# RWKV-5 attention and a mixture of depths on one core: k loads on ScalarE's queue, the first chosen rows a step later, the last rows in parts

## The chip, the cores and the metric

One core of a Trainium2 chip runs the whole program as a single launch. The metric is the device time of that launch in microseconds, the median of several runs; beside it stands one profiled execution, from which all rows below come.

## The reference, cut to what matters

```python
# attention: r, k, v are (B=4, H=8, S=768, D=48), w and u are (8, 48)
for t in range(S):
    cur = einsum('bhd,bhe->bhde', u * k[t], v[t])
    y[t] = einsum('bhd,bhde->bhe', r[t], state + cur)
    state = w * state + einsum('bhd,bhe->bhde', k[t], v[t])
x = y.transpose(0, 2, 1, 3).reshape(B, S, 384)
# mixture of depths, for each batch b
scores = x[b] @ w_gate
top = argpartition(-scores, 128)[:128]            # capacity 128 of 768 rows
ye = maximum(x[b, top] @ w1, 0) @ w2              # 384 -> 1024 -> 384
out[b] = x[b]
out[b, top] = x[b, top] + sigmoid(scores[top])[:, None] * ye
```

## The kernel before

The sequence is cut into units of 128 tokens, six to a batch, 24 in all. A loop over `i` from 1 to 24 is a software pipeline: in step `i` TensorE (PE) finishes the rows of unit `i-1` (`states_part`, `values_part`), makes the state sums and scores of unit `i` (`state_sums`, `scores`) and turns k and r of unit `i+1` with the identity (`turn_k`, `turn_r`). GpSimd (POOL) does four elementwise products in each step (`scaled` of unit `i+2`, `diagonal` of `i+1`, two in `bonus` of `i+2`). VectorE (DVE) masks and sums, ScalarE (ACT) copies PSUM to SBUF (`leave_y`, `turned_k`) and scales the states (`decays`). The order on each engine is the order in which the code is written; no scheduler moves anything.

Loads: `load(n, which)` issues DMAs from HBM. One unit's k or r is one DMA of 192 KB in runs of 192 bytes; v is two DMAs of 96 KB for units 0 to 9 and one after that. Step `i` loads k and r of unit `i+4` and v of unit `i+3`, all on SyncE's queue (SP), which also carries the stores of finished rows (`store_y`, 384 KB for two units). k has four buffers, r four, v five. The expert weights `w1` and `w2` come in eight DMAs of 384 KB on ScalarE's queue in steps 7 to 14 (`weights`).

Mixture of depths: a batch's scores are turned into places by comparisons; `one_hot` and `pick` give the 128 chosen row numbers, `picked` writes them as `idx`, `fetch` gathers the rows from HBM (`xr`, an indirect DMA of POOL), `chosen` turns them on PE, `chosen_copy` brings them to SBUF (`xt`). Then eight `hidden` and eight `expert` pieces are queued, and `pieces(m)` takes `m` of them at three places of each later step (table `FIRST` for batch 0, `STEP` for the others). `leave` makes the gated sum, `store_rows` scatters the rows. For batch 0, `fetch` stands at the end of step 9, and `chosen` near the end of step 10. The last batch has no later steps: its expert runs alone behind the loop, the tail.

The row numbers 0 to 127 that `one_hot` compares with are read from `slots`, columns 384 to 511 of the PSUM bank `PE` (tile `e`), into whose other columns `hidden` writes:

```python
slots = PE[:, Dm : Dm + 128]
nc.vector.tensor_tensor(OH[b, z], q[:, :, None].to_broadcast([128, NC, 128]),
                        slots[:, None, :].to_broadcast([128, NC, 128]), op=OP.is_equal)
```

Of the kernel before, what the change touches and what calls it, by code (L numbers as in the profile page):

```python
# [7 lines left out]
F32 = mybir.dt.float32  # L8
# [9 lines left out]
def kernel(  # L18
# [84 lines left out]
    kpad = const.tile([128, H, PAD], F32, name="kpad")  # L103
    KIN, VIN = {}, {}

    def load(n, which):
        if n >= NU:
            return
        b, c = divmod(n, NC)
        rows = slice(c * T, (c + 1) * T)  # L110
        if "k" in which:
            KIN[n] = kpad[:, :, :D] if n == 0 else work.tile([128, H, D], F32, name="kin", bufs=NIN)
            nc.sync.dma_start(out=KIN[n], in_=k[b, :, rows, :].rearrange("h t d -> t h d"))
        if "r" in which:
# [349 lines left out]

    def one_hot(b, z):
        OH[b, z] = work.tile([128, NC, 128], BF16, name="oh")
        if z:
            q = work.tile([128, NC], F32, name="qz")
            nc.vector.tensor_scalar(q, QQ[b], float(-128 * z), None, op0=OP.add)
        else:  # L470
            q = QQ[b]
        nc.vector.tensor_tensor(OH[b, z], q[:, :, None].to_broadcast([128, NC, 128]),  # L472
                                slots[:, None, :].to_broadcast([128, NC, 128]), op=OP.is_equal)

# [45 lines left out]
    def chosen(b, z):  # L520
        for d in range(KD):
            nc.tensor.transpose(rows_bank(b, z)[:, d * 128 : (d + 1) * 128],
                                XR[b, z][:, d * 128 : (d + 1) * 128], ident)

    def chosen_copy(b, z):
        XT[b, z] = work.tile([128, KD, 128], F32, name="xt", bufs=NST + 1)
        nc.scalar.copy(XT[b, z], rows_bank(b, z)[:, :Dm].rearrange("d (k t) -> d k t", k=KD))  # L527

# [6 lines left out]
    def hidden(b, z, f):  # L535
# [5 lines left out]
        for d in range(KD):  # L541
            nc.tensor.matmul(out=pe[:, (f - f0) * 128 : (f - f0 + 1) * 128], lhsT=w1[:, d, f * 128 : (f + 1) * 128],  # L542
                             rhs=XT[b, z][:, d, :], start=(d == 0), stop=(d == KD - 1))
        if f == f1 - 1:
            nc.scalar.activation(HT[b, z][:, f0:f1, :],
                                 pe[:, : (f1 - f0) * 128].rearrange("f (a t) -> f a t", a=f1 - f0), AF.Relu)

    def expert(b, z, f):
# [50 lines left out]
    NONE = (0, 0, 0)  # L599
    FIRST = NONE, (1, 1, 1), (1, 1, 1), (1, 1, 1), (1, 1, 1), (0, 2, 2)  # L600
    STEP = NONE, (2, 1, 1), (1, 1, 1), (1, 1, 1), (1, 1, 1), (0, 2, 1)
    counts = {}
    for b in range(B - 1):
# [3 lines left out]
        for z in range(NST):  # L607
# [3 lines left out]
            at(e + 4, "pool", fetch, b, z)  # L611
            at(e + 5, "chosen", chosen, b, z)
            at(e + 5, "chosen copy", chosen_copy, b, z)
            at(e + 5, "queue", enqueue, b, z)
            at(e + 5, "gate", gates, b, z)
        for j, m in enumerate(STEP if b else FIRST):
# [21 lines left out]
    nc.vector.tensor_mul(wc, tr[:, 1, :, C], tr[:, 1, :, C])  # L638
    load(3, "kr")
    bonus(0)  # L640
# [176 lines left out]
```

## Time and profile before

| what | value |
|---|---|
| median of 3 runs (lowest to highest) | 171.22 us (170.57 to 174.28) |
| time of the profiled execution | 170.33 us |
| its span, first to last instruction | 168.5 us |
| busy share of the span: PE, DVE, POOL, ACT | 88%, 64%, 62%, 48% |
| DMA: share of the 16 engines, SP's queue (q1) and ACT's (q10) | 51.9% and 6.6% |
| PE clock in the 40 slices | 0.9 or more, but for slices 11 (0.7), 12 (0.8), 15 (0.7) and 16 (0.5), counted from 1: `9999999999789975999999999999999999999998` |

The profiled execution stands 0.89 us below the median, and its span 1.83 us below its own time. Times in rows count from the start of the span. A name such as `SPq` or `ACTq` means the queue's own sequencer, which issues DMAs. Steps are found by their PE instructions: `L361` and `L368` are the state sums, `L319` the scores, `L333` the rows y, `L428` the score transpose that follows them, `L522` the transposes of chosen rows, `L542` a `hidden` piece (six records), `L549` an `expert` piece (two records).

### The profile page before, as it was taken

What the parts mean: (1) busy time and instruction counts of PE and PEld (TensorE: products, weight loads), DVE (VectorE), ACT (ScalarE), POOL (GpSimd) and SP (SyncE); (2) the same over time, 40 slices, a digit from 0 to 9 for tenths busy, and PEclk for the clock granted to TensorE, in tenths of its full rate; (3) what the DMA queues carried; (4) which work ended last, traced back from release to release, by engine and by line L of the source; (5) the groups of instructions that cost most, each with busy time, mean ns of one, the idle gap of its engine ahead of it and who ended that gap; (6) DMA issues with size and microseconds to landing.
All of it is one profiled execution on the core that took longest, in us unless ns stands there. A gap on an engine that the chain in (4) does not pass through costs nothing.

```text
span 168.5 us, 8206 instructions
## 1 busy us (share of the span) xinstructions
PE 147.5 (88%) x3531; PEld 115.2 (68%) x3532; DVE 107.4 (64%) x325; ACT 80.1 (48%) x279; POOL 103.9 (62%) x135
## 2 busy tenths in 40 slices
PE   6899998898598849999999989999998887698970
PEld 2587886686486639888676778877757767558730
DVE  6889888779367681667787766677877656402010
ACT  3286778657255443546455547464555453002200
POOL 7689989888806796178645997876559700022001
PEclk9999999999789975999999999999999999999998
DMA  5997888798999799879977778492201221011001
GB/s 121 173 188 151 176 160 214 141 228 198 239 221 233 180 223 222 209 197 241 297 201 156 144 173 184 91 218 53 92 9 53 97 93 51 2 47 47 4 0 49
DMA packets 81715, 24.33 MB, mean 144 GB/s; under 512 B 75533, under 2 KB 81294, under 8 KB 81678
## 3 DMA queue, kind: packets, MB, share of 16 engines
q1 hardware_dynamic: 78320, 18.88, 51.9%
q10 hardware_dynamic: 2846, 3.35, 6.6%
q0 software_dynamic: 512, 1.57, 3.0%
q8 instruction: 28, 0.46, 1.1%
q14 instruction: 9, 0.07, 0.2%
HBM read 18.29 MB, written 5.51 MB: 141 GB/s over the span
## 4 chain that ended last, share of the span: by engine, by line
PE 42%; issue 23%; POOL 11%; DMA 11%; DVE 4%; SPq 4%; ACT 2%; POOLq 1%; DVEq 0%
PE y L333 9%; PE e L542 7%; PE rp L319 6%; DMA vw<-in_v_dram 5%; PE e L549 4%; PE rp L361 4%; DMA xr<-out_dram,idx 4%; SPq L121 3%; POOL rku L248 2%; PE pk L282 2%; POOL at L263 2%; POOL rk L246 2%; DMA vin<-in_v_dram 2%; PE rp L368 2%; PE pk L278 2%
## 5 line engine op out<-in xcount | busy, mean ns | idle before, releaser
L263 POOL TENSOR_TENSOR at<-dia,du 128x512 f32<-128x512 f32 (+2 forms) x24 | 23.2, 967 | 23.7 <-DVE du L253 13.3
L542 PE MATMUL e<-xt,w 128*128 128x128 f32 x162 | 24.8, 296 | 3.0 <-DVE oh L472 1.3
L248 POOL TENSOR_TENSOR rku<-rk,ub 128x384 f32<-128x384 f32 x24 | 24.1, 1004 | 2.7 <-DMA ub<-in_u_dram 0.9
L542 PEld LDWEIGHTS e<-xt,w 128*128 128x128 f32 x162 | 20.6, 198 | 4.9 <-ACT xt L527 1.4
L246 POOL TENSOR_TENSOR rk<-rpad,kin 128x384 f32<-128x384 f32 x23 | 23.1, 1003 | 0.0
L397 ACT COPY x<-y 128x192 f32<-128x192 f32 x23 | 7.4, 320 | 30.2 <-PE y L333 30.1
L240 POOL TENSOR_TENSOR kw<-kin,wk 128x384 f32<-128x384 f32 x21 | 21.1, 1003 | 0.1
L383 ACT ACTIVATE z<-g,wc 128x48 f32<-128x48 f32 x80 | 20.1, 322 | 0.0
L319 PE MATMUL rp<-rh,kh 48*64 48x64 f32 x768 | 18.4, 232 | 0.8 <-issue 0.7
L319 PEld LDWEIGHTS rp<-rh,kh 48*64 48x64 f32 x768 | 14.8, 141 | 5.5 <-issue 2.5
L333 PEld LDWEIGHTS y<-z,rh 48*64 48x64 f32 x704 | 13.7, 138 | 6.4 <-ACT x L399 1.7
L324 DVE COPY_PREDICATED at<-mask,rp 128x512 f32<-128x512 uint32 x24 | 17.5, 729 | 0.5 <-POOL at L263 0.5
L333 PE MATMUL y<-z,rh 48*64 48x48 f32 x704 | 16.7, 226 | 0.1
L375 DVE TENSOR_TENSOR z<-rp,z 128x192 f32<-128x192 f32 x20 | 7.1, 356 | 15.2 <-PE rp L319 10.7
L501 POOL DMA_INDIRECT xr<-out_dram,idx x4 | 4.1, 1036 | 18.2 <-DVE idx L483 18.2
L253 DVE TENSOR_REDUCE du<-rku 128x8 f32<-128x384 f32 x24 | 13.1, 545 | 2.2 <-POOL rku L248 2.1
L549 PE MATMUL e<-w,ht 128*128 128x384 f32 x32 | 13.7, 526 | 0.3 <-DVE oh L472 0.3
L416 DVE SCALAR_TENSOR_TENSOR scr<-x,m 128x384 f32<-128x384 f32 x24 | 13.1, 548 | 0.7 <-ACT x L399 0.7
L564 POOL DMA_INDIRECT out_dram<-ot,idx x4 | 4.0, 1010 | 15.0 <-DVE ot L555 14.7
L444 DVE TENSOR_SCALAR_CACHE_REDUCE gt<-srow,sc 128x128 bf16<-128x128 f32 (+4 forms) x20 | 12.2, 609 | 0.0
L333 PE MATMUL y<-vin,at 64*64 64x48 f32 x448 | 10.3, 224 | 1.5 <-ACT tiny L346 1.2
L313 DVE TENSOR_TENSOR rh<-pr,tr 128x256 f32<-128x256 f32 x14 | 5.9, 420 | 8.9 <-PE pr L282 8.9
(134 smaller groups left out, 300.9 us busy)
## 6 DMA issues: line engine op xcount, KB each, us to landing
rpad<-in_r_dram SPq DMA_DIRECT2D x24, 192.0 KB, 4.2
kin<-in_k_dram SPq DMA_DIRECT2D x23, 192.0 KB, 4.4
out_dram<-x SPq DMA_DIRECT2D x11, 384.0 KB, 5.1
w<-in_moe_w_dram ACTq DMA_DIRECT2D x8, 384.0 KB, 4.6
vin<-in_v_dram SPq DMA_DIRECT2D x14, 192.0 KB, 4.8
vw<-in_v_dram SPq DMA_DIRECT2D x20, 96.0 KB, 3.4
out_dram<-x SPq DMA_DIRECT2D x2, 192.0 KB
kpad<-in_k_dram SPq DMA_DIRECT2D x1, 192.0 KB
```

What stands on the lines that cost most here:

```text
L240: engine.tensor_mul(kws[n % NKW][:, :, :D], KIN[n], wk)
L246: nc.gpsimd.tensor_mul(rk, rpads[n % NIN][:, :, :D], KIN[n])
L248: nc.gpsimd.tensor_mul(RKU[n], rk, ub)
L253: nc.vector.tensor_reduce(DU[n], RKU[n].rearrange("t (p i) d -> t i p d", i=2), axis=AX.X, op=OP.add)
L263: nc.gpsimd.tensor_mul(AT[n][:, :m], dia[:, None, :].to_broadcast([128, m, C]), DU[n].rearrange("t i p -> t (i p)")[:, :m, None].to_broadc ...
L319: nc.tensor.matmul(out=RP[half(c), i, hp * C : (hp + 1) * C], lhsT=KH[n][head(i), hp, half(c)], rhs=RH[n][head(i), hp, half(c)], start=Tru ...
L324: nc.vector.copy_predicated(at, causal, RP[:, :, : NP * C].rearrange("s i (p t) -> s i p t", p=NP))
L333: nc.tensor.matmul(out=y_out(hp, i, c), lhsT=lhsT, rhs=rhs, start=(n, i, c) not in begun, stop=True, skip_group_check=True)
L383: nc.scalar.activation(state(n + 1)[:, hp, 0, :], G[n][:, hp, :], AF.Copy, scale=wc[:, hp : hp + 1])
L416: nc.vector.scalar_tensor_tensor(scr, X[n], 1.0, wg, op0=OP.mult, op1=OP.mult, accum_out=sc[b][:, c : c + 1])
L542: nc.tensor.matmul(out=pe[:, (f - f0) * 128 : (f - f0 + 1) * 128], lhsT=w1[:, d, f * 128 : (f + 1) * 128], rhs=XT[b, z][:, d, :], start=(d ...
L549: nc.tensor.matmul(out=expert_bank(b, z)[:, :Dm], lhsT=HT[b, z][:, f, :], rhs=w2[:, f, :], start=(f == 0), stop=(f == FB - 1))
```

## The change

Three edits. First, k of units 3 to 14 is loaded on ScalarE's queue instead of SyncE's. In step `i` the issue of k of unit `i+4` stands on ACT behind `decays` and `diagonal_rest` and ahead of the weights and of the copies of `leave_y`; r and v stay on SyncE. k of units 0 to 2 and of 15 to 23 stays on SyncE.

Second, `chosen`, `chosen_copy` and `enqueue` of batch 0 move from the end of step 10 to the middle of step 11, between `scores` and `values_part`; its gate moves to the end of step 11. The table `FIRST` gives one piece less in step 11 and one more in step 15.

Third, the tail. The last `one_hot` reads `count`, the same numbers in SBUF, instead of `slots`. The last chosen rows are turned into two PSUM banks in turn (`pk`, `pr`) and copied as three tiles, two by ACT and one by DVE, ahead of `leaves()` of batch 2. The last `expert` runs as two halves of 192 columns, each of eight matmuls, with a gated sum and a scatter of its own; `last_index` makes the half rows' numbers, 2 x index and 2 x index + 1.

```diff
+    BY_SCALAR = range(3, 15)
...
-            nc.sync.dma_start(out=KIN[n], in_=k[b, :, rows, :].rearrange("h t d -> t h d"))
+            queue = nc.scalar if n in BY_SCALAR else nc.sync
+            queue.dma_start(out=KIN[n], in_=k[b, :, rows, :].rearrange("h t d -> t h d"))
...
-    def one_hot(b, z):
+    def one_hot(b, z, numbers=slots):
...
-                                slots[:, None, :].to_broadcast([128, NC, 128]), op=OP.is_equal)
+                                numbers[:, None, :].to_broadcast([128, NC, 128]), op=OP.is_equal)
...
+    LASTS = PK, PR
...
-            nc.tensor.transpose(rows_bank(b, z)[:, d * 128 : (d + 1) * 128],
-                                XR[b, z][:, d * 128 : (d + 1) * 128], ident)
+            bank = LASTS[d % len(LASTS)] if last(b, z) else rows_bank(b, z)
+            nc.tensor.transpose(bank[:, d * 128 : (d + 1) * 128], XR[b, z][:, d * 128 : (d + 1) * 128], ident)
...
+        if last(b, z):
+            parts = [work.tile([128, 1, 128], F32, name=f"xt{d}", bufs=1) for d in range(KD)]
+            for d in range(KD):
+                bank = LASTS[d % len(LASTS)]
+                from_bank = bank[:, d * 128 : (d + 1) * 128]
+                (nc.vector.tensor_copy if d % 2 else nc.scalar.copy)(parts[d][:, 0, :], from_bank)
+            XT[b, z] = parts
+            return
...
+    def last_expert(b, z, g, f):
+        nc.tensor.matmul(out=(YP0, RP0)[g][:, : Dm // 2], lhsT=HT[b, z][:, f, :],
+                         rhs=w2[:, f, g * Dm // 2 : (g + 1) * Dm // 2], start=(f == 0), stop=(f == FB - 1))
...
-    FIRST = NONE, (1, 1, 1), (1, 1, 1), (1, 1, 1), (1, 1, 1), (0, 2, 2)
+    FIRST = NONE, (0, 1, 1), (1, 1, 1), (1, 1, 1), (1, 1, 1), (1, 2, 2)
...
+            m, first = (e + 5, "") if b else (e + 6, "first ")
+            at(m, first + "chosen", chosen, b, z)
+            at(m, first + "chosen copy", chosen_copy, b, z)
+            at(m, first + "queue", enqueue, b, z)
+            at(m, "gate", gates, b, z)
...
-        load(i + 4, "kr")
+        load(i + 4, "r" if i + 4 in BY_SCALAR else "kr")
...
+            diagonal_rest(i)
+            if i + 4 in BY_SCALAR:
+                load(i + 4, "k")
             if i in PARTS:
                 weights(PARTS.index(i))
-            diagonal_rest(i)
...
+        run(i, "first chosen")
         values_part(i - 1)
+        run(i, "first chosen copy")
+        run(i, "first queue")
...
-        one_hot(b, z)
+        one_hot(b, z, count)
         pieces(2)
...
+        for g in range(2):
+            for f in range(FB):
+                last_expert(b, z, g, f)
+            last_leave(b, z, g)
```

SyncE's queue, the loads of steps 4 and 5 and the store between them (`kin` is k, `rpad` r, `vw` v). Before:

```order
L113 DMA kin<-in_k_dram 128x8x48
L115 DMA rpad_85<-in_r_dram 128x8x48
L121 DMA vw_95<-in_v_dram 64x8x48 x2
L407 DMA out_dram<-x 128x2x384
L113 DMA kin<-in_k_dram 128x8x48
L115 DMA rpad_86<-in_r_dram 128x8x48
```

and in the changed kernel:

```order
L117 DMA rpad_85<-in_r_dram 128x8x48
L123 DMA vw_95<-in_v_dram 64x8x48 x2
L409 DMA out_dram<-x 128x2x384
L117 DMA rpad_86<-in_r_dram 128x8x48
L123 DMA vw_96<-in_v_dram 64x8x48 x2
```

A unit's r and v now follow the r and v of the unit before with no k between them.

ScalarE in the same steps, from the states' decay (`z`) to the next copy of k (`kh`). Before:

```order
L383 ACTIVATE z<-g,wc 128x48 x4
L269 ACTIVATE at<-dia,du 128x64 x2
L397 COPY x<-y 128x4x48
L398 COPY x<-y 64x4x48
L399 COPY x<-y 64x4x48
L306 COPY kh<-pk 128x512
```

and in the changed kernel:

```order
L385 ACTIVATE z<-g,wc 128x48 x4
L271 ACTIVATE at<-dia,du 128x64 x2
L115 DMA kin<-in_k_dram 128x8x48
L399 COPY x<-y 128x4x48
L400 COPY x<-y 64x4x48
L401 COPY x<-y 64x4x48
L308 COPY kh<-pk 128x512
```

The issue of k stands between the diagonal and the copies of y, and everything behind it on ACT waits until it is issued.

TensorE from the end of step 10 into step 11 (`xr` are batch 0's chosen rows, `xt` their copy). Before:

```order
L522 MATMUL e<-ident,xr 128x128 x3
L333 MATMUL y<-z,rh 64x48 x16
L368 MATMUL rp<-vin,kw_92 48x48 x8
L542 MATMUL e<-xt,w_76 128x128 x3
L319 MATMUL rp<-rh,kh 64x64 x16
L333 MATMUL y<-vin,at 64x48 x16
L542 MATMUL e<-xt,w_76 128x128 x3
```

and in the changed kernel:

```order
L335 MATMUL y<-z,rh 64x48 x16
L370 MATMUL rp<-vin,kw_92 48x48 x8
L321 MATMUL rp<-rh,kh 64x64 x16
L526 MATMUL e<-ident,xr 128x128 x3
L335 MATMUL y<-vin,at 64x48 x16
L554 MATMUL e<-xt,w_76 128x128 x3
```

The transposes of the chosen rows stand three groups of matmuls later, and one piece of the first hidden layer less stands in this step.

## Rows read from the trace of the kernel before

**Rows 1.** The chain that ended last, merged: start us, us, what.

```profile
26.57 2.73 SPq L121
35.80 2.66 SPq L121
38.50 5.31 DMA vw<-in_v_dram
...
55.64 5.96 DMA xr<-out_dram,idx
```

**Rows 2.** Timeline of PE, steps 6 to 12: start, us, instruction, [idle before].

```profile
33.38 0.87 PE L361 MATMUL rp<-vw,kw 128*48 128x96 f32 x16 [0.73 <-DMA vw<-in_v_dram]
...
37.45 0.87 PE L361 MATMUL rp<-vw,kw 128*48 128x96 f32 x16
...
39.75 0.32 PE L428 MATMUL m<-ident,sc 128*128 128x128 f32 x1
...
43.95 1.29 PE L361 MATMUL rp<-vw,kw 128*48 128x96 f32 x16 [2.35 <-DMA vw<-in_v_dram]
...
47.71 0.32 PE L428 MATMUL m<-ident,sc 128*128 128x128 f32 x1
...
61.64 0.90 PE L522 MATMUL e<-ident,xr 128*128 128x128 f32 x3 [2.25 <-DMA xr<-out_dram,idx]
62.48 1.11 PE L333 MATMUL y<-z,rh 48*64 48x48 f32 x32
...
68.61 0.27 PE L428 MATMUL m<-ident,sc 128*128 128x128 f32 x1
...
70.27 0.68 PE L333 MATMUL y<-z,rh 48*64 48x48 f32 x32
...
73.96 0.27 PE L428 MATMUL m<-ident,sc 128*128 128x128 f32 x1
```

**Rows 3.** Windows: stretch, its us, busy of each engine, PEclk, DMA share, GB/s.

```profile
28.50:30.00 1.50, 0.87 (x37) 0.65 (x33) 1.40 (x7) 1.34 (x6) 1.29 (x3) 1.00 0.20 43
...
43.90:47.20 3.30, 3.25 (x69) 2.58 (x73) 0.72 (x3) 0.00 (x0) 2.14 (x3) 0.55 0.99 278
...
61.60:68.20 6.60, 6.56 (x124) 5.83 (x125) 2.58 (x10) 2.19 (x9) 4.16 (x5) 0.51 1.01 226
```

**Rows 4.** Timeline of ACT and its queue, steps 5 and 7.

```profile
28.35 1.01 ACT L383 ACTIVATE z<-g,wc 128x48 f32<-128x48 f32 x4
...
37.66 0.33 ACT L383 ACTIVATE z<-g,wc 128x48 f32<-128x48 f32 x1
37.75 0.40 ACTq L223 DMA_DIRECT2D w<-in_moe_w_dram  x1
37.90 0.77 ACT L383 ACTIVATE z<-g,wc 128x48 f32<-128x48 f32 x3
...
39.89 0.32 ACT L397 COPY x<-y 128x192 f32<-128x192 f32 x1 [0.74 <-PE y L333]
```

**Rows 5.** Timeline of DVE, end of step 10.

```profile
60.02 0.42 DVE L313 TENSOR_TENSOR rh<-pk,tr 128x256 f32<-128x256 f32 x1
```

**Rows 6.** DMA issues by line: xcount, median us from issue to landing.

```profile
xr<-out_dram,idx POOLq DMA_INDIRECT x4, 3.3
```

**Rows 7.** Timeline of all engines in the tail.

```profile
144.14 0.95 DVE L472 TENSOR_TENSOR oh<-qq,e 128x768 bf16<-128x768 f32 x1
...
145.15 0.94 PE L542 MATMUL e<-xt,w 128*128 128x128 f32 x6 [1.34 <-DVE oh L472]
...
146.57 0.29 PE L477 MATMUL pr<-tok,oh 128*128 128x2 bf16 x6
...
151.85 0.48 ACT L527 COPY xt<-pk 128x384 f32<-128x384 f32 x1 [5.34 <-PE pk L522]
...
157.84 5.33 PE L549 MATMUL y<-w,ht 128*128 128x384 f32 x16
...
163.28 0.62 DVE L555 SCALAR_TENSOR_TENSOR ot<-y,gate,xr 128x384 f32<-128x384 f32 x1 [10.67 <-PE y L549]
```

More of the change, by code (lines that the diff above doesn't have):

```diff
@@ L521, in chosen @@
         for d in range(KD):
-            nc.tensor.transpose(rows_bank(b, z)[:, d * 128 : (d + 1) * 128],
-                                XR[b, z][:, d * 128 : (d + 1) * 128], ident)
+            bank = LASTS[d % len(LASTS)] if last(b, z) else rows_bank(b, z)
+            nc.tensor.transpose(bank[:, d * 128 : (d + 1) * 128], XR[b, z][:, d * 128 : (d + 1) * 128], ident)
     def chosen_copy(b, z):
-        XT[b, z] = work.tile([128, KD, 128], F32, name="xt", bufs=NST + 1)
-        nc.scalar.copy(XT[b, z], rows_bank(b, z)[:, :Dm].rearrange("d (k t) -> d k t", k=KD))
+        if last(b, z):
[6 more added lines that the diff above has]
+            return
+        xt = work.tile([128, KD, 128], F32, name="xt", bufs=NST + 1)
+        nc.scalar.copy(xt, rows_bank(b, z)[:, :Dm].rearrange("d (k t) -> d k t", k=KD))
+        XT[b, z] = [xt[:, d : d + 1, :] for d in range(KD)]
     def gates(b, z):
@@ L542, in hidden @@
             nc.tensor.matmul(out=pe[:, (f - f0) * 128 : (f - f0 + 1) * 128], lhsT=w1[:, d, f * 128 : (f + 1) * 128],
-                             rhs=XT[b, z][:, d, :], start=(d == 0), stop=(d == KD - 1))
+                             rhs=XT[b, z][d][:, 0, :], start=(d == 0), stop=(d == KD - 1))
         if f == f1 - 1:
@@ L546, in hidden, with last_index, last_leave @@
                                  pe[:, : (f1 - f0) * 128].rearrange("f (a t) -> f a t", a=f1 - f0), AF.Relu)
+    out_halves = out.rearrange("b s (g e) -> (b s g) e", g=2)
+    HALVES = const.tile([128, 2], I32)
+    def last_index(b, z, p):
+        q = work.tile([128, 1], F32, name="qi", bufs=1)
+        nc.vector.tensor_reduce(q, p, axis=AX.X, op=OP.add)
+        with nc.allow_low_precision(reason="whole numbers below 2^24"):
+            for g in range(2):
+                nc.vector.tensor_scalar(HALVES[:, g : g + 1], q, 2.0, float(g), op0=OP.mult, op1=OP.add)
+    def last_expert(b, z, g, f):
+        nc.tensor.matmul(out=(YP0, RP0)[g][:, : Dm // 2], lhsT=HT[b, z][:, f, :],
+                         rhs=w2[:, f, g * Dm // 2 : (g + 1) * Dm // 2], start=(f == 0), stop=(f == FB - 1))
+    def last_leave(b, z, g):
+        m = min(128, cap - z * 128)
+        cols = slice(g * Dm // 2, (g + 1) * Dm // 2)
+        ot = work.tile([128, Dm // 2], F32, name=f"ot{g}", bufs=1)
+        nc.vector.scalar_tensor_tensor(ot, (YP0, RP0)[g][:, : Dm // 2], GA[b, z], XR[b, z][:, cols],
+                                       op0=OP.mult, op1=OP.add)
+        nc.gpsimd.memset(spacer, 0.0)
+        st = nc.gpsimd.indirect_dma_start(
+            out=out_halves[: 2 * (b + 1) * S, :],
+            out_offset=bass.IndirectOffsetOnAxis(ap=HALVES[:m, g : g + 1], axis=0), in_=ot[:m, :], in_offset=None)
+        apart(st.ins, b, z)
+        for o in moves[b, z][1:]:
+            tc.declare_no_dep(st.ins, o.ins, reason="other columns")
+        moves[b, z].append(st)
     def expert(b, z, f):
@@ L611 @@
             at(e + 4, "pool", fetch, b, z)
[L612 to L615, printed above, removed]
+            m, first = (e + 5, "") if b else (e + 6, "first ")
[3 more added lines that the diff above has]
+            at(m, "gate", gates, b, z)
         for j, m in enumerate(STEP if b else FIRST):
@@ L638 @@
     nc.vector.tensor_mul(wc, tr[:, 1, :, C], tr[:, 1, :, C])
-    load(3, "kr")
+    load(3, "r")
     bonus(0)
@@ L650 @@
     diagonal_rest(0)
+    load(3, "k")
     scaled(1, nc.vector)
@@ L659 @@
     turned_k(1)
+    load(4, "k")
     states(0)
@@ L670 @@
     load(3, "v")
-    load(4, "kr")
+    load(4, "r")
     for i in range(1, NU + 1):
-        load(i + 4, "kr")
+        load(i + 4, "r" if i + 4 in BY_SCALAR else "kr")
         load(i + 3, "v")
@@ L772 @@
         fetch(b, z)
+        if last(b, z):
+            last_index(b, z, ENDI)
     pieces(len(queue))
-    leaves()
-    store_rows()
     for z in range(NST):
@@ L778 @@
         chosen_copy(b, z)
-        gates(b, z)
-        enqueue(b, z)
-        pieces(len(queue))
         leaves()
         store_rows()
+        gates(b, z)
+        if not last(b, z):
+            enqueue(b, z)
+            pieces(len(queue))
+            leaves()
+            store_rows()
+            continue
+        for f in range(FB):
+            hidden(b, z, f)
+        for g in range(2):
+            for f in range(FB):
+                last_expert(b, z, g, f)
+            last_leave(b, z, g)
 _INS = ['r', 'k', 'v', 'w', 'u', 'moe_w_gate', 'moe_w1', 'moe_w2', 'moe_capacity']
```

## The prediction

> **What bounds the kernel now.** I read the chain of waits first. From step 5 to step 11 it leaves the engines in three places: twice it runs over an issue on SyncE's queue of 2.7 us and the landing of a v load behind it, and once over the 5.96 us of the gather of batch 0's chosen rows [rows 1]. Elsewhere in the loop it stays mostly on PE. The timeline of PE shows what these cost: waits of 0.73 and 2.35 us for v in steps 6 and 8, and 2.25 us for the gather at the end of step 10 [rows 2]. The windows show a second cost. After the 2.35 us wait the granted clock is 0.55 over 43.9 to 47.2 us, after the 2.25 us wait 0.51 over 61.6 to 68.2 us, so PE ran mostly at 1.2 GHz in place of 2.4 [rows 3]. The same work beside it gives the price. From the state sums to the score transpose PE takes 43.95 to 47.71, 3.76 us, against 37.45 to 39.75, 2.30 us, one step earlier: 1.46 us lost. From the first y group to the score transpose it takes 62.48 to 68.61, 6.13 us, against 70.27 to 73.96, 3.69 us, one step later with the same two hidden pieces: 2.44 us lost [rows 2]. The five together are 0.73 + 2.35 + 1.46 + 2.25 + 2.44 = 9.23 us. The wait of 0.73 us lowered no clock. After step 12 PE is nearly always busy, and the tail is a chain of PE's.
>
> **k on ScalarE's queue.** The question is whether v was late because the DMA engines were full or because SyncE's queue held it up. In the window from 28.5 to 30.0 us the engines are 20% busy and move 43 GB/s [rows 3], while SyncE's queue, until 29.30, is still in the v issue that began at 26.57 [rows 1]. So in this stretch one queue cannot keep enough in flight to feed the engines, and every issue that stands ahead of v delays it. Without k, r and v follow each other directly; a unit then has two loads on SyncE and one on ScalarE, whose queue is separate. Taken whole this returns 0.73 + 2.35 + 1.46 = 4.54 us. The DMA work itself stays, and when two queues are busy the engines are full: share 0.99 and 1.01 in the later windows [rows 3]. From step 7 the weights come on top, so I take 4.0 us; the ends are 0 (v as late as before) and 4.54.
>
> The Trainium skill ("DMA: Bandwidth & Descriptors", section "Issuing engines are not separate DMA queues") states the contrary: initiating DMAs on several engines saves only the sequencer's time, which is usually small, since all run on the same 16 engines. The 20% window speaks against it here; by that rule this term would be 0, which is the first rival.
>
> The cost is on ScalarE, in order: behind each of the twelve k issues wait the copies of y, and behind those the copy of k and the next y group of PE. The nearest rows are the weight issues that stand there already: 0.40 us at 37.75, between two pieces of the z group, which together end 1.01 us after they began, as the four z of step 5 without an issue do (1.01) [rows 4]. The sequencer issued while the engine worked off what it had. And ScalarE then idles 0.74 us for y [rows 4], so an issue up to that length has cover. The low end is 0. The high end is an issue as long as SyncE's v issue, 2.73 us [rows 1]: 2.73 - 0.74 = 2.0 us, twelve times, 24 us. Being k alone, or k and one weight load, on a queue of its own, it is nearest to the weight issue; I take 0.4 us in all, for a few issues that overrun. A gain is excluded, since ScalarE gets work and gives up none.
>
> **The first chosen rows later.** The 2.25 us wait and the 2.44 us of clock behind it, 4.69 us, hang on the transposes of `xr` standing ahead of step 11's y group, state sums and scores. Moved behind the scores, they are reached later. What is late next: the scores need `rh`, whose last half ends at 60.02 + 0.42 = 60.44 us [rows 5], and take about 0.6 us, so PE would come to the transposes at about 61.1 on this clock, and the gather landed at 61.6. A wait of 0.5 us stays, short of the 0.73 that lowered no clock. Term: 4.69 - 0.5 = 4.2 us. Ends: 4.69 if the gather comes quicker (the median of the four is 3.3 us against its 5.96 [rows 1, 6]), and 0 if it lands another 2 us later. ScalarE's copy of the rows and DVE's gate move with the transposes, so they wait less, and POOL is not touched: its four products follow the gather issue as before. The piece that `FIRST` takes from step 11 returns in step 15, zero in sum.
>
> **The tail.** First, PE sat 1.34 us for `one_hot` ahead of a hidden piece that does not need it [rows 7]: both touch the bank `e`, the one by reading `slots`. With `count` in SBUF the piece can start 1.34 us sooner, at 143.81. The hidden and the expert piece take 145.15 to 146.57, 1.42 us, so the pick would be reached at 145.23, and `one_hot` is done at 144.14 + 0.95 = 145.09 [rows 7]. All of 1.34 is saved, and everything behind is PE's. If reading SBUF and PSUM side by side changed the 0.95 by 0.2, the wait would be at most 0.1. Second, the copy of 0.48 us [rows 7] in three parts on two engines: the first hidden matmul needs one part; between 0 and 0.48, and as transposes and copies in one bank may still wait for each other I take 0.3. Third, the halves: the expert's 16 records, 5.33 us [rows 7], become 32 of half the columns. At half the time each that is zero; if the double weight loads show, perhaps 0.2 us more. The gated sum behind it, 0.62 us, is halved at best, 0.31 less; I take 0.2 net, ends -0.2 and 0.31. The first half's scatter goes out under the second half's matmuls; the two number instructions stand on an idle DVE. Together 1.34 + 0.3 + 0.2 = 1.84 us, from 1.0 to 2.1.
>
> **Sum.** 4.0 + 4.2 + 1.84 - 0.4 = 9.6 us. The profiled execution took 170.33 us, so 160.7; the median of the runs shown lies 0.89 us higher, which makes 161.6 us. All good ends together give 4.54 + 4.69 + 2.1 = 11.3, or 159.9.
>
> **The rivals.**
>
> One: the second queue brings nothing. DMA engines bound steps 5 to 10, v comes as late as before, and the waits of 0.73 and 2.35 us stay with their clock. For it speaks the share of 0.99 to 1.01 in the later windows, against it the 0.20 [rows 3]. Then 170.33 - 4.2 - 1.84 + 0.4 = 164.7, at the median 165.6 us.
>
> Two: the chosen rows still stall PE long enough to drop the clock. With k taking its own share, the gather waits behind more traffic and lands 2 us or more later relative to PE. For it: 5.96 us in the busy stretch against a median of 3.3 [rows 1, 6]. Against it: three groups of matmuls now stand ahead. Without that term: 170.33 - 4.0 - 1.84 + 0.4 = 164.9, at the median 165.8 us.
>
> Three, slower: ScalarE is held in the k issues as SyncE is in v. If an issue overruns the 0.74 us of cover by x, PE gets y and k copies late by x in each of twelve steps. The longer steps also take the pressure off the loads, so only 4.2 + 1.84 = 6.0 us of gains are left, and from x = 0.5 us on the kernel is slower. At x = 1.0, half the high end, it is 170.33 - 6.0 + 12 = 176.3, at the median 177.2 us. Against it stand the 0.40 us of the weight issues and their full cover [rows 4].
>
> **How the numbers follow.** The forecast has 0.66: its two large terms rest each on a wait that the trace shows, with the next late thing worked out. Rival one has 0.16, rival two 0.09, the slower one 0.06; 0.03 is left for none of these. Low end: the good ends, 159.9, less 0.7 us of scatter, a little under the 0.65 between the median and the lowest run, rounded to 159.2. High end: beyond rivals one and two at 165.6 and 165.8, with 1.2 us for runs that come out higher, 167.0. That leaves out the slower rival and stragglers. A measurement of this kernel tells a change of about 2% from none, 3.4 us: faster means under 167.8. The forecast and the first two rivals fall there but for a small rest: faster 0.88, within 2% 0.06, slower 0.06.
>
> **What would show it.** In the changed kernel's trace: the v waits of PE in steps 6 and 8 gone or under 0.7 us, and v issues of SyncE shorter; ACT queue's k issues near 0.4 us, the idle time of PE's y group behind ScalarE's copies as small as now; the chosen rows' transposes in step 11 with a wait under 1 us; the granted clock full in all slices of the loop; no wait of PE for `one_hot` in the tail; the two scatters 2.5 to 3 us apart. I am wrong if the DMA share stays near 0.8 with v still late (rival one), if the clock still falls at the chosen rows (two), or if ACT queue's issues last over 1.2 us (three).

## The result, and the profile after

The changed kernel took 167.47 us, the median of four runs (164.90 to 170.83), beside 171.28 us (170.57 to 174.28, four runs) for the kernel before on the same chip: a ratio of 0.9689, 95% interval 0.9602 to 0.9776. So it is faster, by 3.8 us by the medians and by 5.3 us by the ratio. The forecast was 161.6 us, and the range ended at 167.0. The profiled execution of the changed kernel took 168.74 us (span 166.9) and is one of its longer ones. Ratios here are taken from undisturbed runs alone, medians from all runs.

PE's timeline in steps 6 to 11 answers to [rows 2]. The waits for `v` of 0.73 and 2.35 us and the wait of 2.25 us for the gather are gone. Other waits stand in their place:

```profile
34.49 0.33 PE L321 MATMUL rp<-rh,kh 48*64 48x64 f32 x3
35.94 0.69 PE L321 MATMUL rp<-rh,kh 48*64 48x64 f32 x29 [1.13 <-issue]
...
44.07 0.68 PE L321 MATMUL rp<-rh,kh 48*64 48x64 f32 x28
46.08 0.33 PE L321 MATMUL rp<-rh,kh 48*64 48x64 f32 x4 [1.33 <-issue]
...
54.92 0.47 PE L370 MATMUL rp<-vin,kw 64*48 64x48 f32 x18 [0.24 <-DVE idx L485]
56.23 0.34 PE L370 MATMUL rp<-vin,kw 64*48 64x48 f32 x11 [0.84 <-issue]
...
59.23 0.68 PE L335 MATMUL y<-z,rh 48*64 48x48 f32 x30 [0.24 <-ACT x L401]
62.04 0.26 PE L335 MATMUL y<-z,rh 48*64 48x48 f32 x2 [2.13 <-issue]
...
63.50 0.90 PE L526 MATMUL e<-ident,xr 128*128 128x128 f32 x3
```

The new waits cut a group of like matmuls in two: 3 and 29 of the 32 scores, 28 and 4, 18 and 14 of the state sums, 30 and 2 of the y rows. Both parts read and write the same tiles, and the trace names no semaphore ("issue"). They come to 1.13 + 1.33 + 0.84 + 2.13 = 5.43 us, where the waits that went were 5.33. The kernel before has waits for issue too, but short ones: 0.63 us in step 5 and 0.42 in step 10. The transposes of the chosen rows (L526) stand at 63.50 without a wait.

Windows of the same kernel; the first three run from the end of one such wait to the end of another, the last stands behind the wait of 2.13 us (columns as in [rows 3], counts in brackets):

```profile
30.29:35.93 5.64, 4.53 (x126) 3.61 (x126) 4.38 (x16) 3.39 (x13) 5.22 (x6) 1.00 1.06 231
46.08:56.22 10.14, 8.49 (x254) 6.93 (x254) 8.08 (x25) 6.11 (x23) 5.68 (x7) 1.00 0.76 181
56.23:62.03 5.80, 3.43 (x127) 2.60 (x128) 3.88 (x13) 1.80 (x6) 5.68 (x7) 1.00 0.82 206
62.60:69.40 6.80, 6.80 (x100) 5.80 (x96) 2.08 (x5) 3.14 (x11) 2.70 (x3) 0.50 0.69 188
```

PE's matmuls and weight loads in the three add up to 252, 508 and 255. With the few records of PE's sequencer that lie between them (73 in the whole span) that is 256 or twice 256. The last row shows the clock: granted 0.50, PE at 1.2 GHz, for the 6.8 us behind the longest of them, as behind the gather's wait before [rows 3].

Every 256 instructions suggests the program itself. Part 3 of the page, the DMA queues, has a queue for it (packets, MB, share of 16 engines), and part 2 the clock in 40 slices:

```profile
PEclk9999999999999995699999999999999999999997
...
q8 instruction: 28, 0.46, 1.2%
```

28 packets and 0.46 MB are 16 KB each, 28 blocks for the 7,168 records of PE (3547 matmuls, 3548 weight loads, 73 of its sequencer): one block holds about 256 instructions. Where was the block when PE waited 2.13 us? The DMA view of 56.3 to 59.4 us, ahead of that wait, and of 59.4 to 60.6 us, around its beginning:

```profile
q10 hardware_dynamic: 1430, 0.58, 67.4%
q1 hardware_dynamic: 911, 0.17, 28.9%
```

```profile
q8 instruction: 1, 0.02, 5.4%
```

In the first stretch ScalarE's and SyncE's loads fill the engines and no instruction packet runs. One runs from 59.49 to 60.53 us, when most of them are through, and PE goes on at 62.04, 1.5 us behind its end. That the loads held the packet up is so far only read from this order.

ScalarE's queue, k and the weight load behind it, answers to [rows 4]:

```profile
39.94 0.37 ACTq L115 DMA_DIRECT2D kin<-in_k_dram  x1
40.35 0.88 ACTq L225 DMA_DIRECT2D w<-in_moe_w_dram  x1
```

The k issues take 0.37 to 0.43 us, the weight issues behind them up to 1.13. SyncE's longest single `v` issue takes 1.96 us (at 33.72) in place of the 2.73 of [rows 1], so they are shorter in this execution, as the prediction said; in after_again below one takes 2.84. The tail, all engines, answers to [rows 7]:

```profile
145.13 0.96 DVE L474 TENSOR_TENSOR oh<-qq,count 128x768 bf16<-128x768 f32 x1
...
146.14 0.30 PE L479 MATMUL pr<-tok,oh 128*128 128x2 bf16 x6
150.91 0.27 PE L526 MATMUL pk<-ident,xr 128*128 128x128 f32 x1
...
151.75 2.27 PE L554 MATMUL e<-xt,w 128*128 128x128 f32 x18 [0.35 <-ACT xt L534]
157.21 2.77 PE L572 MATMUL y<-w,ht 128*128 128x192 f32 x16
...
160.78 0.98 POOL L582 DMA_INDIRECT out_dram<-ot,HALVES  x1 [7.28 <-DVE ot L579]
162.69 0.42 DVE L579 SCALAR_TENSOR_TENSOR ot<-rp,gate,xr 128x192 f32<-128x192 f32 x1 [2.18 <-PE rp L572]
163.38 0.96 POOL L582 DMA_INDIRECT out_dram<-ot,HALVES  x1 [1.53 <-DVE ot L579]
```

`one_hot` runs beside PE's pieces, and the wait of 1.34 us is gone. The two scatters stand 2.6 us apart.

For all that follows I measure stretches of PE between the score transposes (L428 before, L430 after) of two steps, read from the timelines. Each number is one profiled execution; the last column runs from the last score transpose (142.23 before, 143.28 after) to the end of the span.

| kernel (us) | steps 5 to 8 | 8 to 11 | 11 to 12 | 14 to 15 | tail |
|---|---|---|---|---|---|
| before | 16.9 | 20.9 | 5.3 | 5.78 | 26.3 |
| after | 15.3 | 19.6 | 6.6 | 7.70 | 23.6 |
| k_only | 14.4 | 20.4 | 5.9 | 5.79 | 27.9 |
| chosen_only | 16.0 | 17.5 | 6.6 | 7.70 | 27.7 |
| tail_only | 14.5 | 22.9 | 5.8 | 5.78 | 23.7 |
| no_k | 14.5 | 17.4 | 6.2 | 9.35 | 23.6 |
| after_again | 15.8 | 18.5 | 6.2 | 7.70 | 23.6 |
| no_k_again | 15.6 | 16.3 | 6.3 | 7.70 | 23.7 |
| k_early | 14.7 | 20.6 | 6.3 | 7.70 | 23.6 |
| shift | 12.8 | 17.6 | 7.2 | 7.70 | 23.6 |
| shift_again | 12.8 | 19.3 | 6.3 | 7.70 | 23.6 |
| shift_no_k | 13.3 | 17.2 | 6.0 | 7.70 | 23.7 |
| no_weights | 14.7 | 15.3 | 6.3 | 7.70 | 23.7 |
| more_loads | 15.2 | 22.3 | 6.5 | 7.70 | 23.6 |

### The profile page after: what moved, and what is told of

It is laid out like the page before. It is cut to its first block, busy times and chain, and to the rows that moved or that the text cites. A ratio compares the mean times of both kernels' runs of the same rounds, so it can differ in the third digit from the quotient of the medians.

```text
span 166.9 us, 8245 instructions
## 1 busy us (share of the span) xinstructions
PE 146.6 (88%) x3547; PEld 116.7 (70%) x3548; DVE 108.5 (65%) x330; ACT 80.4 (48%) x280; POOL 105.1 (63%) x137
## 4 chain that ended last, share of the span: by engine, by line
PE 56%; issue 12%; POOL 10%; DVE 7%; DMA 5%; ACT 4%; SPq 2%; POOLq 1%; DVEq 0%
PE y L335 13%; PE e L554 9%; PE rp L321 6%; PE rp L363 4%; PE rp L591 3%; DMA vw<-in_v_dram 3%; PE e L591 2%; POOL rku L250 2%; POOL at L265 2%; DMA kin<-in_k_dram 2%; POOL rk L248 2%; PE pk L284 2%; PE rp L370 2%; PE pr L280 2%; PE pk L280 2%
## 5 line engine op out<-in xcount | busy, mean ns | idle before, releaser
L265 POOL TENSOR_TENSOR at<-dia,du 128x512 f32<-128x512 f32 (+2 forms) x24 | 23.2, 965 | 21.9 <-DVE du L255 16.3
L554 PEld LDWEIGHTS e<-xt,w 128*128 128x128 f32 x162 | 20.9, 201 | 3.3 <-ACT ht L557 1.0
L399 ACT COPY x<-y 128x192 f32<-128x192 f32 x23 | 7.3, 319 | 26.3 <-PE y L335 26.1
L321 PEld LDWEIGHTS rp<-rh,kh 48*64 48x64 f32 x768 | 14.5, 137 | 6.9 <-issue 4.4
L326 DVE COPY_PREDICATED at<-mask,rp 128x512 f32<-128x512 uint32 x24 | 17.5, 731 | 0.5 <-POOL at L265 0.4
L377 DVE TENSOR_TENSOR z<-rp,z 128x192 f32<-128x192 f32 x20 | 7.1, 356 | 12.8 <-PE rp L321 8.3
L370 PE MATMUL rp<-vin,kw 64*48 64x48 f32 x400 | 9.4, 208 | 1.9 <-issue 1.6
```

Source lines behind the costliest of these rows:

```text
L265: nc.gpsimd.tensor_mul(AT[n][:, :m], dia[:, None, :].to_broadcast([128, m, C]), DU[n].rearrange("t i p -> t (i p)")[:, :m, None].to_broadc ...
L321: nc.tensor.matmul(out=RP[half(c), i, hp * C : (hp + 1) * C], lhsT=KH[n][head(i), hp, half(c)], rhs=RH[n][head(i), hp, half(c)], start=Tru ...
L326: nc.vector.copy_predicated(at, causal, RP[:, :, : NP * C].rearrange("s i (p t) -> s i p t", p=NP))
```

## The experiments

The theory that came out of the traces: where the load waits go, the next late thing is the block of PE's own instructions, so k's place is worth nothing. Rivals: k's gain is real and masked by something else; or something else in those groups holds PE.

### Each part alone, and the change without k

One chip, four runs each; the kernel before on it took 172.75 us (168.14 to 177.59, seven runs).

**k_only** takes the second and third edit back (the rest of the tail's edit, left out here, goes back too):

```diff
-    FIRST = NONE, (0, 1, 1), (1, 1, 1), (1, 1, 1), (1, 1, 1), (1, 2, 2)
+    FIRST = NONE, (1, 1, 1), (1, 1, 1), (1, 1, 1), (1, 1, 1), (0, 2, 2)
...
-            m, first = (e + 5, "") if b else (e + 6, "first ")
+            m, first = e + 5, ""
...
-        one_hot(b, z, count)
+        one_hot(b, z)
```

> The kernel before with k of units 3 to 14 on ScalarE's queue alone. Theory A (PE waits for its own instructions: in the changed kernel's trace PE stands still inside groups of matmuls, 0.27 to 2.13 us at a time, each time a multiple of 256 records after the last, and the two loaded queues delay what it waits for): the two v waits of 0.73 and 2.35 us vanish, but new waits put down to issue, over 0.3 us each and 2 us or more in sum up to step 10, take their place; 1 to 3 us faster, 168.3 to 170.3. Theory B (the forecast's own term): 4.0 us faster, about 167.3, no such waits. Theory C (the second queue brings nothing): v waits as before, 171.3 within 0.7.

Measured: 173.35 us (171.55 to 176.07), no gain. Theory A's waits came, 0.58 + 0.86 + 1.11 = 2.55 us, but not its gain of 1 to 3 us. PE's waits for `v` are gone; those for instructions and the gather are there:

```profile
34.99 0.69 PE L321 MATMUL rp<-rh,kh 48*64 48x64 f32 x29 [0.58 <-issue]
44.80 0.33 PE L321 MATMUL rp<-rh,kh 48*64 48x64 f32 x4 [0.86 <-issue]
...
55.21 0.34 PE L370 MATMUL rp<-vin,kw 64*48 64x48 f32 x11 [1.11 <-issue]
59.20 0.55 PE L526 MATMUL e<-ident,xr 128*128 128x128 f32 x3 [1.23 <-DMA xr<-out_dram,idx]
```

In the tail of this run the `one_hot` wait of 1.34 us (at 145.64) is followed by a lower clock, in the window

```profile
146.00:149.40 3.40, 3.40 (x16) 2.30 (x15) 0.16 (x1) 0.38 (x1) 0.51 (x1) 0.50 0.00 0
```

which makes its tail 27.9 us where the kernel before had 26.3.

**chosen_only** keeps the second edit alone (the tail's other lines are again left out):

```diff
-    BY_SCALAR = range(3, 15)
+    BY_SCALAR = range(0)
...
-        one_hot(b, z, count)
+        one_hot(b, z)
```

> The kernel before with batch 0's chosen rows a step later alone. Theory A: the load of the queues is as before, so the wait of 2.25 us for the gather goes without issue waits of over 1 us in its place; 3 to 4.5 us faster, 166.8 to 168.3. Theory B: 4.2 us faster, 167.1. Theory D (the clock falls after the v waits and the gather is late whatever stands before it): under 1.5 us faster, clock still 0.5 behind step 10.

Measured: 174.77 us (171.42 to 178.72), no gain that shows. The wait at the chosen rows fell to 0.49 us (61.94, where [rows 2] has 2.25), and steps 8 to 11 took 17.5 us in place of 20.9. But steps 11 to 12 and 14 to 15 became longer by 1.2 and 1.9 us, and its tail lost clock like k_only's. PE waits for `v` here, 0.69, 0.81 and 1.45 us in steps 6 to 8, and behind the chosen rows the granted clock is 0.50 from 62.7 to 66.1 us. Of the three theories D comes nearest.

**tail_only** keeps the third edit alone:

```diff
-    BY_SCALAR = range(3, 15)
+    BY_SCALAR = range(0)
...
-    FIRST = NONE, (0, 1, 1), (1, 1, 1), (1, 1, 1), (1, 1, 1), (1, 2, 2)
+    FIRST = NONE, (1, 1, 1), (1, 1, 1), (1, 1, 1), (1, 1, 1), (0, 2, 2)
...
-            m, first = (e + 5, "") if b else (e + 6, "first ")
+            m, first = e + 5, ""
```

> The kernel before with the tail's edits alone. All theories: 1.0 to 2.1 us faster, about 169.5; PE no longer waits 1.3 us for the one-hot; expert halves take 5.3 to 5.5 us together.

Measured: 169.28 us (168.71 to 170.55), 3.5 us under the kernel before by the medians, with a tail of 23.7 in place of 26.3 us. That is more than the 1.0 to 2.1 us expected, but the kernel before spreads over 9.5 us on this chip, and its fastest run is below all four of these. Its loop is that of the kernel before, k on SyncE, and yet in steps 5 to 8 PE waits for no `v`:

```profile
45.93 0.33 PE L321 MATMUL rp<-rh,kh 48*64 48x64 f32 x4 [1.61 <-issue]
...
63.30 0.55 PE L526 MATMUL e<-ident,xr 128*128 128x128 f32 x3 [3.46 <-DMA xr<-out_dram,idx]
```

The `v` waits of [rows 2] are thus not of every execution: no_k and no_k_again below have none either, chosen_only had three. The wait for instructions is at the place it has in the changed kernel, 28 scores and 4.

**no_k** leaves the first edit out alone (chosen rows and tail as changed):

```diff
-    BY_SCALAR = range(3, 15)
+    BY_SCALAR = range(0)
```

> The changed kernel with all k back on SyncE's queue, so chosen rows later and tail. Theory A: 165 to 166.5, as fast as the changed kernel (about 166) or faster, and with less spread between runs. Theory B: 165.3, which is 4 us slower than the changed kernel was forecast to be; measured against the changed kernel's real time, B asks that it be slower than that by about 4 us, so about 170.

Measured: 168.38 us (164.64 to 172.65), between what theory A and theory B had, and 0.9 us under tail_only. That is what the chosen rows are worth here, within the spread.

### Is k's place worth anything?

On another chip (before: 172.42 us, 168.81 to 176.56, eleven runs), six runs each: the changed kernel again, no_k again (the diff above), and **k_early**:

```diff
-    BY_SCALAR = range(3, 15)
+    BY_SCALAR = range(3, 11)
```

> The changed kernel once more, beside the next kernel on one chip. Theory A (PE's own instructions become the bound: in steps 4 to 11 the fetch of each block of 256 PE instructions ends only 1.2 to 1.6 us before PE can go on, so a load wait that goes is replaced by a wait for instructions): k on ScalarE's queue is worth nothing, this kernel and the one without it agree within 1% (1.7 us). Theory B (the queue's gain of 4 us is real, and was only masked where k was moved alone, by the chosen rows and the tail): this kernel is 2 to 4 us faster than the one without the move. In the trace: PE waits 'for issue' near record counts 1472, 1985, 2497 and 2752 again, 4 to 6 us in all.

> The change without its first part: k of units 3 to 14 stays on SyncE, the chosen rows and the tail as in the changed kernel. Theory A: the same time as the changed kernel within 1%. Theory B: 2 to 4 us slower than the changed kernel.

> k on ScalarE's queue only for units 3 to 10, whose issues stand in steps 1 to 6, before the expert weights start on that queue; units 11 to 14 go back to SyncE. If k and the weights on one queue crowd out PE's instruction fetch, the waits for issue in steps 7 to 11 (1.33, 0.84 and 2.13 us in the changed kernel) halve and the time falls by 1 to 3 us against the changed kernel; if the number of queues doesn't matter (theory A in its plain form, the DMA work is what the fetch stands behind), it is the same within 1%.

Measured: 169.06 (165.73 to 173.65), 169.28 (165.76 to 169.75) and 169.01 us (165.33 to 172.32); k_early against before has the ratio 0.9748, 0.9583 to 0.9913. The three agree within 0.3 us. Theory B, a gain of 2 to 4 us from the queue, falls, and the 1 to 3 us that k_early should give if k and weights on one queue were the harm do not come either.

The traces are less clear. In steps 6 to 11 of after_again the waits for issue are 0.87 + 1.55 + 0.99 = 3.4 us, fewer than the 4 to 6 expected, with none at the state sums; in no_k_again, with k on SyncE, 2.10 us stand at the scores of step 8. In k_early only that one, 1.41 us, is left, as the thought of the harm had it; but there the granted clock is 0.50 from 45.8 to 66.3 us, so PE itself is slower where the others would stand.

### Do the waits follow the count of instructions?

**shift** puts 64 small matmuls, 128 records, at the start; nothing else changes:

```diff
     unread(5, YP[:, 0, :])
+    unread(64, YP[:, 0, :32])
     nc.tensor.transpose(PM[:, :NP], wrow.rearrange("p i d -> p (i d)"), ident[:NP, :NP])
```

> The changed kernel with 64 small matmuls that nobody reads (128 more PE records, a load of weights and a matmul each) ahead of the first transposes. Theory A: the waits for issue come every 256 records at most, so they move by 128 records back in the program: none inside the scores of steps 6 and 8 or at record 2752 of the changed kernel's program, but in the turns of k and r, or the y rows, half a block earlier; counted from the start they stay at 192 and a multiple of 256. Rival (something of these groups themselves, a semaphore the trace does not show or a PSUM bank, holds PE): they stay in the same groups, so their counts move to 64 and a multiple of 256. The time grows by up to 2 us for the added matmuls; only the places count.

Measured: the waits for issue moved.

```profile
31.68 0.32 PE L335 MATMUL y<-vw,at 64*64 64x48 f32 x3 [0.70 <-issue]
36.80 0.54 PE L280 MATMUL pk<-ident,kw 128*112 128x128 f32 x3 [0.40 <-issue]
...
60.05 0.89 PE L335 MATMUL y<-vin,at 64*64 64x48 f32 x22 [0.60 <-issue]
```

They now cut the y rows (29 and 3), the turn of k (1 and 3) and other y rows; none over 0.25 us is left in the scores. Counted from PE's first record, its sequencer's among them, they stand at 1472, 1729 and 3008, in the changed kernel at 1472, 1985, 2497 and 2752: 192 and a multiple of 256 (or one beside it) in both. That they belong to blocks of the program, and not to those groups, is shown. They had also become shorter, and this execution took 164.03 us.

The other traces bear the rule out. In the fourteen together PE has 34 waits for issue of 0.5 us or more: all 34 stand at 192 or 193 and a multiple of 256, and in each PE goes on 1.2 to 1.6 us after a packet of 16 KB on the instruction queue has ended. So at these places PE waits for its program. Shorter ones (0.25 to 0.46 us) also stand elsewhere, as the 0.42 of the kernel before at 2553, and are not counted to it.

### Is that a faster kernel, and does k's place matter then?

Third chip (before: 170.10 us, 167.50 to 173.38, eleven runs), six runs each: shift again, and **shift_no_k**, which is shift with k on SyncE:

```diff
-    BY_SCALAR = range(3, 15)
+    BY_SCALAR = range(0)
```

> The changed kernel with the 64 small matmuls at the start once more, timed. If the one look was typical (issue waits 1.7 us in all in steps 1 to 11 against about 6 in the changed kernel), its median lies 2 to 4 us under the 168 to 169 us of the changed kernel, near 165. Rival (the look was a good run by luck, the sum of the block waits is the same wherever they fall): 168 to 169 us plus up to 1 us for the added matmuls.

> The same 64 small matmuls, but k of units 3 to 14 on SyncE's queue as in the kernel before. Theory A says that PE goes on when the later of two is there, its data or its instructions. Where the shift takes instruction waits away, the waits for v show again: 0.5 to 2 us in steps 6 and 8, and this kernel is 1 to 4 us slower than the one with k on ScalarE's queue and the same matmuls. Rival (the loads are never late enough to matter once the order of chosen rows and tail are as they are): the same time within 1%.

Measured: shift_again 164.42 us (163.69 to 165.46, six runs), ratio to before 0.9727, 0.9663 to 0.9791; shift_no_k 164.90 us (163.14 to 166.35), ratio 0.9681, 0.9594 to 0.9768. By the medians shift is 5.7 us under before on its chip, the changed kernel 3.4 us on the second chip and 3.8 on the first. By the ratio it is not the better: 0.9727 against the changed kernel's 0.9689. The two were not timed on one chip either, so that shift is the faster kernel is not shown. What differs is the spread: its runs lie within 1.8 us, those of the changed kernel within 7.9 (after_again, another chip). Steps 5 to 8 took 12.8 us in both traces of shift, the shortest of all.

k's place again gives nothing measurable: 0.5 us by the medians, by the ratios shift_no_k is even the lower, and the intervals overlap. The expected 1 to 4 us are missed, though one of the expected waits for `v` came, and with it two of over 1 us for instructions, at other blocks than in shift:

```profile
42.23 0.87 PE L363 MATMUL rp<-vw,kw 128*48 128x96 f32 x16 [1.07 <-DMA vw<-in_v_dram]
47.72 0.24 PE L452 MATMUL rp<-ones,gt 128*128 128x1 bf16 x4 [1.59 <-issue]
...
72.07 0.30 PE L370 MATMUL rp<-vin,kw 64*48 64x48 f32 x8 [1.70 <-issue]
```

### Do the loads make the instructions late?

One execution each. **no_weights** leaves out the loads of the expert weights; `w1` and `w2` are filled with 0.01:

```diff
+    nc.gpsimd.memset(w1, 0.01)
+    nc.vector.memset(w2, 0.01)
...
-            if i in PARTS:
-                weights(PARTS.index(i))
```

> The changed kernel without the eight loads of the expert weights; w1 and w2 are filled with 0.01 at the start instead, so the experts compute with other numbers. Theory A: the fetch of PE's instructions no longer stands behind 3.1 MB in steps 7 to 14; the waits for issue at records 1985, 2497 and 2752 (1.33, 0.84 and 2.13 us in the changed kernel) fall to under 0.4 us each. The one at 1472, ahead of the first weights, stays (0.3 to 1.2). Rival (the instructions are late for a reason on PE's own side, whatever the loads do): all stay within 0.5 us of the changed kernel's.

Measured: 167.66 us, with a longer start (the first state sums at 12.51 us in place of 8.98). The waits between 30 and 66 us:

```profile
34.62 0.20 PE L372 MATMUL rp<-vw,kw 64*48 64x48 f32 x1 [0.90 <-issue]
...
39.99 0.69 PE L323 MATMUL rp<-rh,kh 48*64 48x64 f32 x29 [0.85 <-issue]
...
49.80 0.33 PE L323 MATMUL rp<-rh,kh 48*64 48x64 f32 x4 [1.00 <-issue]
```

The wait of 2.13 us at the y rows is gone, the one of 0.84 at the state sums too; 0.41 us stand in the scores behind it, not at a block's end. But the one at 28 scores and 4 stays at 1.00 (1.33 in the changed kernel), and the one at the state sums of step 5 grew from 0.34 to 0.90. Steps 8 to 11 take 15.3 us, the shortest of all kernels and at the full clock; steps 5 to 8 do not gain. That fits theory A, but it does not show that the weights were the cause: with all the weights loaded, after_again has no wait at the state sums and 0.99 us at the y rows, no_k and no_k_again have 0.59 and 0.51 us there, and chosen_only has neither.

**more_loads** adds five loads of 384 KB in steps 16 to 20:

```diff
+    spare = const.tile([128, KD, F // 4], F32)
...
+            if 16 <= i < 21:
+                nc.scalar.dma_start(out=spare, in_=moe_w1[:, : F // 4].rearrange("(kd p) f -> p kd f", p=128))
```

> The changed kernel with five more loads of 384 KB on ScalarE's queue, one in each of steps 16 to 20, into a tile that nobody reads. Theory A: waits for issue of 0.5 to 2 us appear inside PE's groups in steps 16 to 21, at records 192 and a multiple of 256 (4288 to 5568), where the changed kernel has none over 0.45 us. Rival (instruction blocks are late only in the units up to 10 with their 6 groups of many small matmuls): none appear there.

Measured: 171.45 us, and no wait for issue of over 0.25 us in steps 16 to 21, though the engines are fuller. The window 100 to 110 us of this kernel, where the changed kernel has a DMA share of 0.65 and 140 GB/s:

```profile
100.00:110.00 10.00, 9.23 (x240) 7.90 (x236) 7.25 (x24) 5.62 (x20) 8.87 (x11) 1.00 0.91 230
```

So the theory falls in its plain form: in this execution a DMA share of 0.91 did not by itself make PE's instructions late. Its longer time comes from steps 8 to 11 (22.3 us, with the granted clock at 0.50 from 50 to 70 us), ahead of the added loads.

## Why the prediction was right in sign and too large in size

**k on ScalarE's queue: the step that failed.** The prediction said that, taken whole, the move returns 0.73 + 2.35 + 1.46 = 4.54 us, and took 4.0. What the move does came as said: no wait for `v` in steps 6 and 8, k issues near 0.4 us, ScalarE not held. The time did not come: 173.35 against 172.75 us alone, 169.06 against 169.28 with the rest, 164.42 against 164.90 with the shift; steps 5 to 8 take 15.1 us on the mean of the five kernels with k on ScalarE, the weights and no shift, 15.5 on the mean of the five with k on SyncE. Three things were wrong in it. First, "what is late next" was asked for the gather, but not for `v`: PE's next block of instructions was nearly as late, in the middle of the scores that follow the very wait of 2.35 us. In the kernel before that block's packet ended at 42.26 us; an estimate from the 1.2 to 1.6 us above has PE ready to go on at 43.5 to 43.9, so with `v` in time it would still have stood 0.5 to 0.9 us there. Waits of over 0.25 us for `v` and for instructions come together to 2.0 us in steps 5 to 8 on the mean of those five kernels with k on ScalarE, all for instructions, and to 2.4 on that of the five with k on SyncE, where they are for `v` in two (3.1 and 3.0 us) and for instructions in three (1.6, 1.9 and 2.4). One wait took the place of the other.

Second, the 2.35 us came from one execution; tail_only, no_k and no_k_again have the same loads in steps 5 to 8 without it. Third, the window with a share of 0.20, which spoke against rival one, is the last part of one `v` issue. In its first part, and during the wait of 2.35 us, the engines were full (the kernel before, columns as in [rows 3]):

```profile
26.57:28.50 1.93, 1.93 (x56) 1.66 (x55) 1.42 (x3) 1.86 (x7) 1.85 (x3) 1.00 1.12 256
...
41.00:43.80 2.80, 0.59 (x32) 0.47 (x32) 2.68 (x8) 2.03 (x8) 2.57 (x4) 1.00 1.14 207
```

Rival one had the right outcome for this term, with the wrong reason: `v` does come in time in all eight traces with k on ScalarE.

By the Trainium skill ("DMA: Bandwidth & Descriptors", section "Issuing engines are not separate DMA queues") several issuing engines save only sequencer time, which is usually small. The time agrees: nothing was gained.

**ScalarE's cost.** 0.4 us was taken; the issues of 0.37 to 0.43 us cost nothing that a wait shows (PE's 0.24 us for ScalarE's copies at 59.23 stand in step 11, which issues no k there). The slower rival, issues that hold ScalarE, did not come.

**The chosen rows: the wait went, two other waits came.** The gather's wait fell to 0 to 0.9 us, as forecast, and steps 8 to 11 take 18.3 us on the mean of the six kernels with the edit and without shift or other loads, 21.4 us on the mean of the three without: 3.1 less, of which 0.9 to 1.6 us is the hidden piece that left step 11 (0.94 us at the full clock, 1.65 at the lower, at which it ran in the kernel before). Against that stand two steps of the prediction that failed. It said that the piece which returns in step 15 is "zero in sum". It stands there at the first place, ahead of the scores, and writes the bank `e` while batch 1's `one_hot` reads `slots` from it. The changed kernel, all engines, step 15:

```profile
87.46 0.95 DVE L474 TENSOR_TENSOR oh<-qq,e 128x768 bf16<-128x768 f32 x1
88.46 0.91 PE L591 MATMUL e<-w,ht 128*128 128x384 f32 x2 [0.62 <-DVE oh L474]
89.31 0.69 PE L321 MATMUL rp<-rh,kh 48*64 48x64 f32 x32
```

and the kernel before, where scores and y rows run under that `one_hot`:

```profile
88.10 0.66 PE L319 MATMUL rp<-rh,kh 48*64 48x64 f32 x32
88.46 0.95 DVE L472 TENSOR_TENSOR oh<-qq,e 128x768 bf16<-128x768 f32 x1
88.58 0.63 PE L333 MATMUL y<-vin,at 64*64 64x48 f32 x32
89.47 1.56 PE L549 MATMUL e<-w,ht 128*128 128x384 f32 x4 [0.26 <-DVE oh L472]
```

Step 14 to 15 takes 7.70 us in ten of the eleven traces with the edit (9.35 in no_k, where a wait of 1.11 us for instructions and the lower clock come on top), 5.78 without it: 1.92 more, of which the piece itself is 0.9. It is the clash that the tail edit removes for the last batch.

And it said that ScalarE's and DVE's work on the chosen rows, moved along, would wait less. The gate's sum now stands on DVE behind the work of step 11, and ScalarE, in order, waits for it with the copies of the next step behind. From shift_again:

```profile
67.51 0.55 DVE L543 SCALAR_TENSOR_TENSOR scr<-xr,m 128x384 f32<-128x384 f32 x1
...
68.11 0.20 ACT L545 ACTIVATE gate<-gsum 128x1 f32<-128x1 f32 x1 [2.16 <-DVE scr L543]
...
68.33 0.15 ACT L348 COPY tiny<-y 1x1 f32<-1x1 f32 x1
...
68.63 0.68 PE L335 MATMUL y<-vin,at 64*64 64x48 f32 x32 [0.43 <-ACT tiny L348]
```

ScalarE idles 2.16 us, and PE 0.43 of them, as in five other traces with the edit. Steps 11 to 12 take 6.4 us on the mean of the six kernels with the edit, 5.7 on that of the three without. The sum: 3.1 - 0.7 - 1.9 = 0.5 us, where 4.2 were forecast; no_k against tail_only gave 0.9. Both are rough, since steps 8 to 11 alone range from 16.3 to 20.6 us over the six executions with the edit. The clock was expected full in all slices. It is not: the longest wait for instructions (2.13 us) now stands where the gather's wait stood, with the same 6.8 us at 1.2 GHz behind it.

**The tail: right, and larger.** 26.3 to 23.6 us, and 23.6 or 23.7 in every kernel with the edit: 2.7 us for the 1.84 forecast. From the last score transpose to the pick 4.34 became 2.86 us (1.48 for 1.34); from the rows' transpose to the first hidden matmul 1.06 became 0.84 (0.22 for 0.3); the expert in halves cost nothing (5.44 and 5.48 us up to the last sum); from the last sum to the last scatter's issue 0.90 became 0.69. The missing part is behind it. The last scatter of the kernel before is

```profile
164.18 0.98 POOL L564 DMA_INDIRECT out_dram<-ot,idx  x1 [10.67 <-DVE ot L555]
```

4.4 us before the end of the span; in the changed kernel 163.38 to 166.9 leaves 3.5 us. The prediction gave the smaller last scatter nothing; it and the end behind it are worth 0.8. The stretch can be worth more: k_only and chosen_only, without the edit, lost another 1.4 to 1.6 us to the clock behind the wait for `one_hot`.

**The sum.** Measured by stretches: 2.7 for the tail, 0.5 for the chosen rows, 0.4 for k, 3.6 us in all, where the medians differ by 3.8 and the ratio gives 5.3. The forecast was 9.6. The 2.7 is firm; 0.5 and 0.4 are differences of means that scatter by more than themselves, so that the sum comes near the medians is in part luck.

**What stays open.** What makes the blocks late, mostly in steps 4 to 11 and seldom behind them (the longest 1.70 us in step 13 of shift_no_k; 0.72 in step 21 of no_k, no_k_again and k_early). At the scores of steps 6 and 8 it is not the weights, since no_weights has these waits too; at the 2.13 us wait the weights may be the cause, which one execution cannot show; and k, r and v could not be taken away. Open too is why the clock stays at 0.50 between steps 5 and 12 for 20.5 us in k_early and 23.9 in more_loads, and not at all in no_weights. That shift spreads less because its blocks end at better places is argued from the traces, not separated from its 64 matmuls at the start or from its chip. Not tried: a step 15 without the piece at its first place, or `one_hot` from `count` for all batches, which by the rows above should return about 1 us.

## What to carry to other kernels

When a wait is removed, list everything that the engine needs next, its own instructions among them: a wait "for issue" in the middle of a group of like matmuls, at a constant count from the last one, is the program itself arriving late, and moving the loads between queues did not end it here. A unit of work that is moved "zero in sum" has to be checked at its new place for the banks it shares with another engine and for what stands behind it on in-order queues. Waits of a loop in one profiled execution should be looked for in a second one before they are summed.

## What the runs showed of the hardware

PE's instructions come as DMA packets of 16 KB on a queue of their own, one for about 256 records, and PE stood still up to 2.13 us for one, until 1.2 to 1.6 us after the packet's end. The Trainium skill ("Runtime: NRT & Kernel Launch", section "Instruction fetch mechanics") has blocks of that size and count, which these traces bear out, and calls the cost of crossing one "mostly hidden". Here most crossings were hidden, but not all: 5.4 us in steps 6 to 11 of the changed kernel, 0 to 3.4 in the thirteen other traces. 64 matmuls that nobody reads, 1.7 us of PE's time at the start, went with a narrower spread (1.8 us over six runs); that they make the kernel faster is not shown.
